# One-hot routing tables in fp16 with the columns innermost, slot lines by rounding, and a new written order, in a fused attention and mixture-of-experts kernel

## The chip, the cores and the metric

The kernel runs on one core of a Trainium2 chip. The metric is the device time of one execution in microseconds (us). TensorE is called PE here, VectorE DVE, ScalarE ACT, GpSimd POOL, and SyncE SP, as in the profile.

## The reference

Eight sequences of 576 tokens go through windowed attention with a linear bias, then through a mixture of eight experts of which each token uses two.

```python
# attention: B, H, S, D = 8, 8, 576, 64, window 128
scores = scale * q @ k.T + slopes * -abs(rel)      # masked outside 0 <= rel < 128
attn = softmax(scores)
x = (attn @ v).reshape(B * S, H * D)               # 4608 x 512
# mixture of experts: E, F = 8, 1024
noisy = x @ w_gate + log1p(exp(x @ w_noise)) * noise
top2 = argpartition(-noisy, 2)[:, :2]
top2_w = softmax of the two
for e in range(E):
    for k in range(2):
        mask = top2[:, k] == e
        h = maximum(x[mask] @ w1[e], 0)
        out[mask] += top2_w[mask, k] * (h @ w2[e])
```

## The kernel before

**Attention and routing.** For each batch of 576 tokens the kernel makes scores of 64-row blocks on PE (line 598), the biased minimum on DVE (line 604), the exponentials on ACT (line 612), transposes on PE (line 619) whose results ACT and DVE copy out (lines 301 and 305, tile pT), and the product with v on PE (line 636). When a batch's attention is done, `route(b)` takes its gate logits, finds the two best experts of each token (lines 850 and 854), ranks the tokens within each expert by a matmul with a triangular matrix (lines 858 and 860), and gives each pair of token and expert a slot number. Slots are kept in lines of 64. To write the token numbers to their slots, `tables` makes two one-hot tables for the 10 pairs (5 token rows times 2 experts) of each partition: one over 80 line numbers (line 893), one over 64 columns (line 897), the second multiplied by the token number (line 901). `list_` adds up ten matmuls of one by the other (line 905), and `scatter` adds the 80x64 result to a list in DRAM. `halves` splits a slot number into line and column by an integer shift and a mask (lines 871 to 875), `next_lines` does the same for the next batch (lines 878 to 881).

**Experts.** Inputs and weights are split into a high and a low fp16 part, and each product is three fp16 matmuls. The first two experts start early: a first wave of blocks (256, 256, 256 and 192 slots of each) is computed as soon as the routing of 2, 4, 6 and 7 batches is complete. The second wave does the rest: the last 256 slots of experts 0 and 1, then experts 2 to 7 in blocks of 512, 512 and up to 192 slots, the 512 ones with seven half-size products in place of eight (lines 1459 and 1496 up, 1659 and 1664 down). Their partial products are copied to tiles named side. Weights of later experts are read, their magnitude is taken (line 1204, ACT), and they are split (lines 301, 303 and 1290) while earlier experts run.

**The order.** No engine chooses its work at run time: each engine's instructions stand in a fixed order. That order is made by a planner inside the kernel (class `Order`) which plays the program through with a cost in us for each piece of work (the first number in `dve(0.98, rank, ...)`) and, of the pieces that are ready on an engine, takes the one with the lowest rank. On PE a piece that keeps the matmul shape of the one before it gets a bonus `STAY`. Work that two engines can do (`either`) goes to the one that is free first, the second at a rank later by an entry of `LATE`. The ranks come from the constants at the top of the file: an attention step of unit t (0 to 159) has rank t plus an entry of `STAGE`, a step of the first wave lies between `FFN0` and `FFN1`, one of the second wave at 1000 and above. A strand that waits for a buffer takes it from a ring, also by rank.

Of the kernel before, what the change touches and what calls it, by code (L numbers as in the profile page):

```python
# [8 lines left out]
F32 = mybir.dt.float32  # L9
# [13 lines left out]
NQ = 5  # L23
# [6 lines left out]
LINE, SPAN = 64, 10  # L30
LINES = 88
# [16 lines left out]
ZERO = 2019.65  # L48
LOAD = 1075.19
VALUES = 1169.98  # L50
GATE = (413.12, 503.1)
GATES = -311.61
ROUTE = -79.16
SCATTER = (-1036.89, -486.7, 213.65)
FFN0, FFN1 = 288.77, 555.18
WEIGHTS = ((918.12, 272.55), (959.66, -236.26))
SEQUENCE = ((0, 0), (0, 1), (1, 0), (1, 1), (0, 2), (1, 2), (0, 3), (1, 3))
TOKENS = -394.6
STAGE = (538.41, 414.48, -338.92, -406.83, 42.73, -373.27, 193.47, -830.41)
MIDDLE = 1630.44  # L60
RESULT = -868.28
WEIGHTS_LATE = 1656.15
SOON = -776.11
LISTED = (36.01, -1817.29)
BIG, PARTS = 1971.78, 542.82
TIGHT = (1, 5, 7)
LATE = (964.06, -1700.75, 837.67, 233.39, 327.65, -1019.18, -417.1, -852.6, 26.68, -922.38, 2132.47, 749.7, 255.16, 538.12)
# [4 lines left out]
REST = -38.3  # L72
PACE = (68.65, -27.38)
HOLD = (-376.19, 197.8)
AHEAD = 1022.78
GATHER_LAG, SCATTER_LAG, LISTED_LAG, TURN_LAG = 4.4, 5.0, 3.0, 4.0
STAY, TURN = -339.23, 0.13
TICK, WARM = 3.413, 1.28
LARGEST = 470.85
# [40 lines left out]
class Order:  # L120
# [141 lines left out]
def attention_moe(ctx: ExitStack, tc: tile.TileContext, qk_, v, vt_, w_gate, w_noise, noise, w12,  # L262
# [83 lines left out]
    steps_ = const.tile([128, E * SPAN], F16, name="steps")  # L346
    numbers = const.tile([128, NQ], F32, name="numbers")
# [8 lines left out]
    lines_ = const.tile([128, 2, E], I32, name="lines")  # L356
# [31 lines left out]
    def set_ups():  # L388
# [9 lines left out]
        def counts_():  # L398
            for t, pattern, first_, step in ((steps_, [[1, E * SPAN]], 0, 0), (numbers, [[64, NQ]], 1, 1),
                                             (spare, [[0, 3], [128, 4]], N, 1), (mine, [[-SPAN, E]], 0, 1)):  # L400
# [325 lines left out]
    def divided(k, low, high, r7):  # L726

        b, y, z = k // NP, k // 2, k % 2
        den = yield (denr, r7)
        if not z:  # L730
            xs_[y] = yield (xr, r7)
            mark(opened[y])
        yield opened[y]
        if not k % NP:
            lts[b] = yield (ltr, r7)
            mark(logged[b])
        yield logged[b]
# [90 lines left out]
    lo_ = ap_.tile([128, NQ, 2], I32, name="lo")  # L828
    si = ap_.tile([128, NQ, 2], I32, name="si")
    hot = [ap_.tile([128, 2 * NQ, c], F16, name=f"hot{c}") for c in (E * SPAN, LINE)]  # L830
# [3 lines left out]
    def route(b):  # L834
# [7 lines left out]
        yield act(0.09, rank, lambda: nc.scalar.activation(u, lg[:, :, 8:16], AF.Abs))  # L842
# [3 lines left out]
        yield act(0.1, rank, lambda: nc.scalar.activation(positive, lg[:, :, 8:16], AF.Relu), False)  # L846
# [18 lines left out]

        def slot_numbers():
            with nc.allow_low_precision(reason="whole numbers below 2^24"):
                V.tensor_reduce(si, oh, axis=AX.X, op=OP.add)

        def halves():  # L870
            V.tensor_scalar(both_i, si, 6, None, op0=OP.arith_shift_right)
            V.tensor_scalar(si, si, LINE - 1, None, op0=OP.bitwise_and)
            V.tensor_copy(d, both_i)
            V.scalar_tensor_tensor(ef, ef, float(SPAN), d, op0=OP.mult, op1=OP.add)
            V.tensor_copy(d, si)

        def next_lines():
            V.tensor_copy(lines_[:, 0], base)
            V.tensor_scalar(lines_[:, 1], lines_[:, 0], 6, None, op0=OP.arith_shift_right)
            V.tensor_copy(line, lines_[:, 1])  # L880
            V.scalar_tensor_tensor(rest_of_line, line, -float(LINE), base, op0=OP.mult, op1=OP.add)
# [7 lines left out]
        def tables(eng, z):  # L889

            if z == 0:
                shape = [128, 2 * NQ, E * SPAN]
                eng.tensor_tensor(hot[0], ef.rearrange("p i k -> p (i k)")[:, :, None].to_broadcast(shape),
                                  steps_[:, None, :].to_broadcast(shape), op=OP.is_equal)
            elif z == 1:
                shape = [128, 2 * NQ, LINE]
                eng.tensor_tensor(hot[1], d.rearrange("p i k -> p (i k)")[:, :, None].to_broadcast(shape),
                                  steps_[:, None, 0:LINE].to_broadcast(shape), op=OP.is_equal)
# [16 lines left out]
        r5, both_i = rk[:, 0:NQ], lo_  # L915
        G = V if b == B - 1 else nc.gpsimd
        rest = [
            (0.09, lambda: V.scalar_tensor_tensor(y_, u, 1.0, y_, op0=OP.subtract, op1=OP.subtract)),
# [9 lines left out]
            (0.39, best), (0.39, where),  # L928
            (0.08, lambda: V.tensor_add(ef, idx[:, :, 0:2], inval)),
            (0.15, lambda: V.tensor_tensor(oh, ef[:, :, :, None].to_broadcast([128, NQ, 2, E]),  # L930
# [20 lines left out]
            (0.5, halves)]  # L951
        onward = [(0.3, next_lines), (0.25, next_places)]
# [26 lines left out]
        yield act(0.1, rank, lambda: nc.scalar.activation(d[:, :, 0], d[:, :, 0], AF.Exp))  # L979
# [11 lines left out]
        yield dve(0.98, rank, lambda: tables(nc.vector, 0))  # L991
        yield dve(0.8, rank, lambda: tables(nc.vector, 1))
        if b == B - 1:
            yield dve(0.8, rank, lambda: tables(nc.vector, 2))
        else:
            yield Op((("POOL", 1.55, rank), ("DVE", 0.8, rank + LATE[10])), lambda g: tables(engine[g], 2), slows=0.4)
        a = yield (tb, rank)
        yield pe(0.4, rank, lambda: list_(a))
        yield dve(0.3, rank, lambda: whole_numbers(a))
# [273 lines left out]
    def difference(o, a, b, op, rank):  # L1273
        return dve(0.08 + o.shape[-1] * 0.00112, rank, lambda: nc.vector.tensor_tensor(o, a, b, op=op))  # L1274
# [70 lines left out]
    def wide_pair(blk, j, xa, xb, tt, end, rank):  # L1345
# [28 lines left out]
        yield dve(1.3, rank, powers)  # L1374
# [19 lines left out]
    def piece(blk, j, q, x, up_, rank, done, lows=None):  # L1394
        c = x.shape[-1]
# [3 lines left out]
        yield dve(0.07 + 0.00115 * c, rank, lambda: nc.vector.scalar_tensor_tensor(lo, x, up_, hi, op0=OP.mult, op1=OP.subtract))  # L1399
# [71 lines left out]
    def ups_of(steps, ranks):  # L1471
        for (blk, f), rank in zip(steps, ranks):
# [10 lines left out]
            us = 3 * (blk.n / 2400 + 0.005)  # L1483
# [192 lines left out]
    def downs_of(steps, ranks):  # L1676
        for (blk, f), rank in zip(steps, ranks):
# [12 lines left out]
            if blk.flip:  # L1690
                for c in range(4):
                    end = yield pe(3 * (blk.n / 2400 + 0.005), rank, lambda: mm2_flipped(blk, f, c, ev[2]), False)
# [374 lines left out]
```

## Time and profile before

| what | value |
|---|---|
| median of 3 runs | 1023.29 us (1021.52 to 1024.88) |
| the profiled execution, its own time | 1020.78 us |
| its span, first to last instruction | 1018.9 us |
| PE busy | 979.8 us (96%), 9734 matmuls |
| DVE busy | 796.2 us (78%), 2733 instructions |
| ACT busy | 564.3 us (55%) |
| POOL busy | 331.0 us (32%) |
| mean granted PE clock | 0.993 |

All durations are of the one profiled execution. Busy time of PE is the union of its matmuls with modelled ends, so a busy PE is not one at its peak; idle PE is certain. "x <- y" in a group of instructions is tile written from tiles read.

### The profile page before, as it was taken

How to read it: one execution, taken by the hardware profiler on the slowest of the kernel's cores; microseconds unless marked ns; L12 is line 12 of the kernel's file. 1: busy time of each engine (PE TensorE's matmuls, PEld its weight loads, DVE VectorE, ACT ScalarE, POOL GpSimd, SP SyncE). 2: the span in 40 equal slices, each digit the busy share in tenths (PEclk: the TensorE clock that was granted, in tenths of full speed). 3: DMA queues.
4: the chain of work that ended last, by engine and by line, in shares of the span. 5: the costliest groups of instructions: out<-in, count | busy, mean ns of one | idle time of the engine just before them, and what ended most of it. 6: DMA issues, size and time to landing. Idle time of an engine off the chain costs nothing.

```text
span 1018.9 us, 25787 instructions
## 1 busy us (share of the span) xinstructions
PE 979.8 (96%) x9734; PEld 701.8 (69%) x9734; DVE 796.2 (78%) x2733; ACT 564.3 (55%) x1367; POOL 331.0 (32%) x442
## 2 busy tenths in 40 slices
PE   7999999999899999979999999999999999999997
PEld 4776777776666689657668666856767686666774
DVE  6989989798997633987799598959978995998240
ACT  6977678485535424664567555634665655544221
POOL 1079432343834224321324142404331232321013
PEclk9999999999999999999999999999999999999999
DMA  8999999794149455895559474949693676638024
GB/s 315 410 312 318 312 336 328 236 295 73 42 93 243 76 81 90 162 218 134 94 109 217 104 130 91 226 74 171 97 236 59 151 147 166 108 65 127 4 40 52
DMA packets 175534, 166.59 MB, mean 164 GB/s; under 512 B 128928, under 2 KB 139248, under 8 KB 175408
## 3 DMA queue, kind: packets, MB, share of 16 engines
q1 hardware_dynamic: 157888, 125.59, 45.9%
q0 software_dynamic: 17520, 39.34, 21.8%
q8 instruction: 77, 1.26, 0.5%
q14 instruction: 49, 0.40, 0.1%
HBM read 95.11 MB, written 40.91 MB: 133 GB/s over the span
## 4 chain that ended last, share of the span: by engine, by line
PE 79%; DVE 13%; POOL 2%; DMA 2%; issue 2%; ACT 1%; SPq 0%; POOLq 0%; DVEq 0%; ACTq 0%
PE bank L1659 31%; PE bank L1496 18%; PE bank L1459 12%; PE bank L636 5%; PE bank L1664 4%; PE bank L598 3%; PE bank L619 3%; DVE bhl L1611 1%; DVE p L604 1%; DMA qk<-in_qk_dram 1%; DVE side L1599 1%; DVE held L1290 1%; POOL held L1287 1%; DVE x L748 1%; DVE pT L305 1%
## 5 line engine op out<-in xcount | busy, mean ns | idle before, releaser
L1659 PE MATMUL bank<-held,bhh 128*128 128x512 f16 x734 | 218.4, 379 | 2.6 <-ACT bhh L1618 2.6
L1496 PE MATMUL bank<-bx,held 128*128 128x256 f16 x1824 | 210.5, 273 | 6.8 <-ACT side L301 6.3
L1796 POOL DMA_INDIRECT out_dram<-yo,ix x58 | 96.0, 1655 | 338.0 <-ACT yo L301 281.6
L1496 PEld LDWEIGHTS <-held 128*128 128x128 f16 x1824 | 178.7, 98 | 33.2 <-issue 8.2
L1659 PE MATMUL bank<-held,bhl 128*128 128x512 f16 x367 | 139.1, 379 | 1.5 <-DVE bhl L1611 1.5
L1659 PEld LDWEIGHTS <-bhh 128*128 128x128 f16 x784 | 75.8, 98 | 88.9 <-ACT bhh L1618 4.1
L1459 PE MATMUL bank<-ax,held 128*128 128x256 f16 (+6 forms) x1380 | 133.9, 252 | 2.0 <-DVE ahl L1650 1.5
L1459 PEld LDWEIGHTS <-held 128*128 128x128 f16 x1380 | 115.8, 98 | 17.7 <-issue 3.8
L612 ACT ACTIVATE p<-p,nm 128x192 f32<-128x192 f32 (+2 forms) x288 | 103.7, 427 | 22.4 <-DVE nm L604 21.6
L301 ACT ACTIVATE xt<-xg,fit 128x512 f16<-128x512 f32 (+5 forms) x93 | 62.6, 677 | 60.3 <-DVE fit L1366 27.2
L1618 ACT ACTIVATE bhh<-side 128x512 f16<-128x512 f32 x69 | 42.4, 627 | 94.8 <-DVE side L1599 93.2
L604 DVE CUSTOM_DVE_ANT_0 p<-bank,bias 128x192 f32<-128x192 f32 (+2 forms) x288 | 81.8, 327 | 5.5 <-PE bank L598 4.8
L301 ACT ACTIVATE held<-held,wsc 128x512 f16<-128x512 f32 x93 | 63.3, 713 | 28.9 <-DVE held L1274 14.3
L636 PE MATMUL bank<-vraw,pT 64*64 64x81 f32 (+1 forms) x2048 | 76.7, 240 | 1.6 <-DVE pT L305 0.6
L636 PEld LDWEIGHTS bank<-vraw,pT 64*64 64x64 f32 (+1 forms) x2048 | 68.5, 137 | 10.2 <-issue 2.0
L1338 POOL DMA_INDIRECT xg<-xs_dram,ix x48 | 51.8, 1080 | 70.6 <-DVE xt L1399 36.8
L619 PE MATMUL bank<-ident,p 128*128 128x128 f32 x416 | 68.1, 286 | 6.3 <-ACT pT L301 2.8
L1659 PEld LDWEIGHTS <-bhl 128*128 128x128 f16 x392 | 38.3, 98 | 48.9 <-DVE bhl L1611 2.9
L598 PE MATMUL bank<-qk 64*64 64x192 f32 (+2 forms) x1152 | 65.7, 326 | 6.5 <-DMA qk<-in_qk_dram 5.1
L1290 DVE SCALAR_TENSOR_TENSOR held<-held,wsc,held 128x512 f16<-128x512 f32 x96 | 70.9, 767 | 0.0
L1204 ACT ACTIVATE junk<-held 128x512 bf16<-128x512 f32 x104 | 65.1, 626 | 6.2 <-DMA held<-in_w_dram 4.3
L619 PEld LDWEIGHTS bank<-ident,p 128*128 128x128 f32 x416 | 45.7, 142 | 32.3 <-ACT pT L301 7.6
(284 smaller groups left out, 1793.1 us busy)
## 6 DMA issues: line engine op xcount, KB each, us to landing
held<-in_w_dram SPq DMA_DIRECT2D x61, 512.0 KB
qk<-in_qk_dram SPq DMA_DIRECT2D x31, 576.0 KB
vraw<-in_v_dram SPq DMA_DIRECT2D x16, 810.0 KB
out_dram<-xg SPq DMA_DIRECT2D x10, 1024.0 KB
vt<-in_vt_dram SPq DMA_DIRECT2D x16, 576.0 KB
xs_dram<-x SPq DMA_DIRECT2D x16, 320.0 KB
xs_dram<-x SPq DMA_DIRECT2D x16, 256.0 KB
bx<-xt SPq DMA_TRANSPOSE x96
```

Source lines behind the costliest of these rows:

```text
L301: nc.scalar.activation(o, i, AF.Copy, **kw)
L598: nc.tensor.matmul(s[j % 2][half:half + 64, o:o + c], qk[rows, j * 64:j * 64 + 64], qk[rows, k1 - c:k1], start=True, stop=True)
L604: nc.vector.tensor_tensor_reduce(out=p[:, place(j):place(j) + c], in0=s[z][:, o:o + c], in1=bias4[:, g, z, 192 - c:192], scale=-0.125, sca ...
L612: nc.scalar.activation(pv, pv, AF.Exp, bias=nm[:, z:z + 1], scale=-1.0)
L619: nc.tensor.transpose(t[:, z * 128:z * 128 + 128], p[:, a * 128:a * 128 + 128], ident)
L636: nc.tensor.matmul(o[z * 64:z * 64 + 64, c:c + VC], pt[rows, slot, from_:from_ + 64], t[rows, block, hh], start=(o is first_, z) not in be ...
L1204: nc.scalar.activation(junk, raws_flat(t, z), AF.Abs, accum_out=wam[:, e % 2, z, f:f + 1])
L1290: nc.vector.scalar_tensor_tensor(lo, t, sc, hi, op0=OP.mult, op1=OP.subtract)
L1459: nc.tensor.matmul(t[:, 0:blk.n], wp[:, c], blk.x[:, x + c, 0:blk.n], start=c == 0 and z == 0, stop=c == 3 and z == 2)
L1496: nc.tensor.matmul(t[:, a % 2 * HALF:a % 2 * HALF + HALF], wp, blk.x[:, x], start=first_, stop=False, skip_group_check=True)
L1659: nc.tensor.matmul(blk.y[j][0:r], h[:, cs], wp, start=f == 0 and m == 0, stop=f == 7 and m == 2)
L1796: ins = nc.gpsimd.indirect_dma_start(out=out, out_offset=bass.IndirectOffsetOnAxis(ap=blk.ix[0:r, j:j + 1], axis=0), in_=t[0:r, 0:DM], in_ ...
```

## The change

**Tables.** `row` and `col`, the line and column number of each pair, are now fp16, and so are the counting table `steps_` and the token numbers; the counting table is held expanded over the ten pairs (800 elements where it was 80). The pair index becomes the innermost axis of the tables, `[128, c, 10]` where it was `[128, 10, c]`, so that both inputs of the compare are contiguous on it, and the ten matmuls of `list_` read their operands with a step of ten elements. **Slot lines.** The line of a slot is found by adding and subtracting 1.5 x 2^23 in fp32, with no integers: four instructions per batch where there were five, and three where there were four for the next batch. **Order.** Nearly all rank constants change, and the planner's costs of many pieces (the factor 1.03 on late DVE work goes, too).

```diff
+WHOLE = 1.5 * 2.0 ** 23
-FFN0, FFN1 = 288.77, 555.18
+FFN0, FFN1 = 985.65, 988.51
-STAGE = (538.41, 414.48, -338.92, -406.83, 42.73, -373.27, 193.47, -830.41)
+STAGE = (762.91, 398.43, -692.29, -873.25, -99.37, -122.48, 294.62, -1402.25)
-STAY, TURN = -339.23, 0.13
+STAY, TURN = -180.73, 0.13
...
-        elif e == "DVE" and self.now > FFN1:
-            us *= 1.03
...
-    steps_ = const.tile([128, E * SPAN], F16, name="steps")
-    numbers = const.tile([128, NQ], F32, name="numbers")
+    steps_ = ap_.tile([128, E * SPAN, 2 * NQ], F16, name="steps")
+    numbers = const.tile([128, NQ, 2], F16, name="numbers")
...
+    row, col = (ap_.tile([128, 2 * NQ], F16, name=name) for name in ("row", "col"))
+    hot = [ap_.tile([128, c, 2 * NQ], F16, name=f"hot{c}") for c in (E * SPAN, LINE)]
...
+        def whole_lines(o, i):
+            V.tensor_scalar(o, i, 1.0 / LINE, 0.5 / LINE - 0.5, op0=OP.mult, op1=OP.add)
+            V.tensor_scalar(o, o, WHOLE, WHOLE, op0=OP.add, op1=OP.subtract)
...
         def halves():
-            V.tensor_scalar(both_i, si, 6, None, op0=OP.arith_shift_right)
-            V.tensor_scalar(si, si, LINE - 1, None, op0=OP.bitwise_and)
-            V.tensor_copy(d, both_i)
-            V.scalar_tensor_tensor(ef, ef, float(SPAN), d, op0=OP.mult, op1=OP.add)
-            V.tensor_copy(d, si)
+            row_, col_ = (x.rearrange("p (i k) -> p i k", k=2) for x in (row, col))
+            whole_lines(ln, si)
+            V.scalar_tensor_tensor(row_, ef, float(SPAN), ln, op0=OP.mult, op1=OP.add)
+            V.scalar_tensor_tensor(col_, ln, -float(LINE), si, op0=OP.mult, op1=OP.add)
...
         def next_lines():
-            V.tensor_copy(lines_[:, 0], base)
-            V.tensor_scalar(lines_[:, 1], lines_[:, 0], 6, None, op0=OP.arith_shift_right)
-            V.tensor_copy(line, lines_[:, 1])
+            whole_lines(line, base)
...
+            if z < 2:
+                shape = list(hot[z].shape)
+                eng.tensor_tensor(hot[z], (row, col)[z][:, None, :].to_broadcast(shape), steps_[:, 0:shape[1]], op=OP.is_equal)
             else:
-                h = hot[1].rearrange("p (i k) c -> p i (k c)", k=2)
-                eng.tensor_tensor(h, h, numbers[:, :, None].to_broadcast([128, NQ, 2 * LINE]), op=OP.mult)
+                eng.tensor_tensor(hot[1], hot[1], numbers.rearrange("p i k -> p (i k)")[:, None, :].to_broadcast([128, LINE, 2 * NQ]),
+                                  op=OP.mult)
...
-                nc.tensor.matmul(a[0:E * SPAN, 0:LINE], hot[0][:, z], hot[1][:, z], start=z == 0, stop=z == 2 * NQ - 1)
+                nc.tensor.matmul(a[0:E * SPAN, 0:LINE], hot[0][:, :, z], hot[1][:, :, z], start=z == 0, stop=z == 2 * NQ - 1)
...
-        yield dve(0.98, rank, lambda: tables(nc.vector, 0))
-        yield dve(0.8, rank, lambda: tables(nc.vector, 1))
+        yield dve(0.55, rank, lambda: tables(nc.vector, 0))
+        yield dve(0.45, rank, lambda: tables(nc.vector, 1))
```

## Rows read from the trace of the kernel before

**Rows 1.** Windows by stage; columns: stretch, its length, busy time (instructions) by engine, clock, DMA.
```profile
0.00:10.00 10.00, 4.94 (x62) 3.14 (x62) 6.06 (x35) 7.22 (x19) 3.26 (x23) 1.00 0.70 216
10.00:20.00 10.00, 7.95 (x84) 5.26 (x78) 7.26 (x46) 6.14 (x17) 0.14 (x1) 0.83 1.02 360
20.00:300.00 280.00, 267.73 (x4187) 197.91 (x4186) 249.65 (x1283) 190.41 (x548) 128.56 (x199) 0.99 0.81 259
300.00:440.00 140.00, 140.00 (x1143) 105.20 (x1142) 89.80 (x278) 63.44 (x154) 43.33 (x49) 1.00 0.63 130
440.00:460.00 20.00, 13.86 (x100) 10.18 (x99) 17.97 (x52) 14.03 (x34) 5.47 (x5) 0.91 0.97 218
460.00:1006.00 546.00, 539.99 (x4125) 375.00 (x4124) 425.08 (x1043) 281.87 (x593) 145.64 (x160) 1.00 0.62 119
1006.00:1019.00 13.00, 5.32 (x50) 5.07 (x47) 0.37 (x2) 1.22 (x3) 4.60 (x6) 0.87 0.64 85
```

**Rows 2.** Windows, the ten of 20 to 300 us with most idle PE, one and their sum.
```profile
260.00:270.00 10.00, 8.54 (x108) 6.19 (x106) 9.67 (x39) 6.28 (x15) 9.52 (x10) 1.00 0.27 61
...
sum 100.00, PE 89.33 PEld 65.08 DVE 94.67 ACT 70.38 POOL 58.85; mean PE 8.93 PEld 6.51 DVE 9.47 ACT 7.04 POOL 5.89
```

**Rows 3.** Waits of PE from 20 to 300 us: us in total, times, longest.
```profile
PE bank L619 <- ACT pT L301: 2.8, 6, 0.8
PE bank L619 <- DVE pT L305: 2.4, 4, 1.1
```

**Rows 4.** Timeline at 444 to 453 us: start, us, engine, line, operation.
```profile
444.62 0.62 ACT L1204 ACTIVATE junk<-held 128x512 bf16<-128x512 f32 x1
...
445.79 1.47 PE L1496 MATMUL bank<-bx,spare 128*128 128x256 f16 x12
...
450.06 0.63 ACT L1204 ACTIVATE junk<-held 128x512 bf16<-128x512 f32 x1
...
452.12 1.06 ACT L301 ACTIVATE side<-bank 128x512 f32<-128x512 f32 x2
...
452.75 2.71 PE L1496 MATMUL bank<-bx,held 128*128 128x256 f16 x12 [5.48 <-ACT side L301]
```

**Rows 5.** The tile hot: duration in ns, least, median, most.
```profile
L893 DVE TENSOR_TENSOR hot<-ef,steps x8: 975/982/1919, 76.7 to 299.8; 128x800 f16<-128x800 f32 x8
L897 DVE TENSOR_TENSOR hot<-d,steps x8: 761/816/973, 78.9 to 301.5; 128x640 f16<-128x640 f32 x8
L901 POOL TENSOR_TENSOR hot<-hot,numbers x6: 1254/1256/1256, 81.3 to 247.3; 128x640 f16<-128x640 f16 x6
L901 DVE TENSOR_TENSOR hot<-hot,numbers x2: 818/818/818, 283.3 to 302.9; 128x640 f16<-128x640 f16 x2
```

**Rows 6.** DVE groups by line and shape, 0 to 330 us: busy us, mean ns.
```profile
L871 DVE TENSOR_SCALAR lo<-si 128x10 int32<-128x10 int32 x8 | 2.6, 327 | 0.2
...
L875 DVE CAST d<-si 128x10 f32<-128x10 int32 x8 | 2.0, 252 | 0.3
...
L872 DVE TENSOR_SCALAR si<-si 128x10 int32<-128x10 int32 x8 | 1.8, 230 | 0.3
...
L873 DVE CAST d<-lo 128x10 f32<-128x10 int32 x8 | 1.7, 207 | 0.0
...
L874 DVE SCALAR_TENSOR_TENSOR ef<-ef,d 128x10 f32<-128x10 f32 x8 | 1.4, 171 | 0.3
```

**Rows 7.** Timeline of PE at 85 us, the ten products of one list.
```profile
85.27 0.54 PE L905 MATMUL bank<-hot,hot 128*80 128x64 f16 x10
```

**Rows 8.** Timeline of POOL at the start.
```profile
2.68 0.21 POOL L401 IOTA steps<- 128x80 f16 x1
```

**Rows 9.** Windows at the hand-over and at two later changes of expert.
```profile
450.00:460.00 10.00, 7.25 (x53) 5.85 (x53) 8.11 (x24) 5.60 (x13) 2.24 (x2) 0.83 0.95 203
550.00:560.00 10.00, 8.22 (x67) 6.21 (x64) 9.49 (x29) 8.54 (x23) 4.04 (x3) 1.00 1.17 227
...
930.00:940.00 10.00, 8.42 (x41) 3.54 (x39) 9.06 (x23) 3.61 (x7) 0.00 (x0) 1.00 0.41 79
```

More of the change, by code (lines that the diff above doesn't have):

```diff
@@ L71 @@
 DMA_LAG = 4.0
[L72 to L75, printed above, removed]
+REST = -113.98
+PACE = (44.6, -12.0)
+HOLD = (24.18, 221.19)
+AHEAD = 776.98
 GATHER_LAG, SCATTER_LAG, LISTED_LAG, TURN_LAG = 4.4, 5.0, 3.0, 4.0
-STAY, TURN = -339.23, 0.13
+STAY, TURN = -180.73, 0.13
 TICK, WARM = 3.413, 1.28
-LARGEST = 470.85
+LARGEST = 2707.67
 WIDES, SIDE = 4, 4
@@ L398, in counts_ @@
         def counts_():
-            for t, pattern, first_, step in ((steps_, [[1, E * SPAN]], 0, 0), (numbers, [[64, NQ]], 1, 1),
+            for t, pattern, first_, step in ((steps_, [[1, E * SPAN], [0, 2 * NQ]], 0, 0), (numbers, [[64, NQ], [0, 2]], 1, 1),
                                              (spare, [[0, 3], [128, 4]], N, 1), (mine, [[-SPAN, E]], 0, 1)):
@@ L841, in route @@
         positive = oh2.rearrange("p i k e -> p (i k e)")[:, 0:NQ * E].rearrange("p (i e) -> p i e", e=E)
-        yield act(0.09, rank, lambda: nc.scalar.activation(u, lg[:, :, 8:16], AF.Abs))
+        yield act(0.18, rank, lambda: nc.scalar.activation(u, lg[:, :, 8:16], AF.Abs))
         yield act(0.13, rank, lambda: nc.scalar.activation(y_, u, AF.Exp, scale=-1.0))
@@ L845, in route @@
         yield act(0.13, rank, lambda: nc.scalar.activation(l, u, AF.Ln), False)
-        yield act(0.1, rank, lambda: nc.scalar.activation(positive, lg[:, :, 8:16], AF.Relu), False)
+        yield act(0.18, rank, lambda: nc.scalar.activation(positive, lg[:, :, 8:16], AF.Relu), False)
         def best():
@@ L927, in route @@
         choose = [
-            (0.39, best), (0.39, where),
-            (0.08, lambda: V.tensor_add(ef, idx[:, :, 0:2], inval)),
-            (0.15, lambda: V.tensor_tensor(oh, ef[:, :, :, None].to_broadcast([128, NQ, 2, E]),
+            (0.39, best), (0.62, where),
+            (0.13, lambda: V.tensor_add(ef, idx[:, :, 0:2], inval)),
+            (0.25, lambda: V.tensor_tensor(oh, ef[:, :, :, None].to_broadcast([128, NQ, 2, E]),
                                            iota8[:, None, None, :].to_broadcast([128, NQ, 2, E]), op=OP.is_equal)),
@@ L950, in route @@
             (0.2, slot_numbers),
-            (0.5, halves)]
-        onward = [(0.3, next_lines), (0.25, next_places)]
+            (0.75, halves)]
+        onward = [(0.5, next_lines), (0.5, next_places)]
         def chain(steps, wait):
@@ L978, in route @@
         end = yield pe(0.2, rank, ranks, False)
-        yield act(0.1, rank, lambda: nc.scalar.activation(d[:, :, 0], d[:, :, 0], AF.Exp))
+        yield act(0.2, rank, lambda: nc.scalar.activation(d[:, :, 0], d[:, :, 0], AF.Exp))
         yield end
@@ L990, in route @@
         spawn(gates_out(b, rank))
-        yield dve(0.98, rank, lambda: tables(nc.vector, 0))
-        yield dve(0.8, rank, lambda: tables(nc.vector, 1))
+        yield dve(0.55, rank, lambda: tables(nc.vector, 0))
+        yield dve(0.45, rank, lambda: tables(nc.vector, 1))
         if b == B - 1:
-            yield dve(0.8, rank, lambda: tables(nc.vector, 2))
+            yield dve(0.45, rank, lambda: tables(nc.vector, 2))
         else:
-            yield Op((("POOL", 1.55, rank), ("DVE", 0.8, rank + LATE[10])), lambda g: tables(engine[g], 2), slows=0.4)
+            yield Op((("POOL", 1.55, rank), ("DVE", 0.45, rank + LATE[10])), lambda g: tables(engine[g], 2), slows=0.4)
         a = yield (tb, rank)
         yield pe(0.4, rank, lambda: list_(a))
-        yield dve(0.3, rank, lambda: whole_numbers(a))
+        yield dve(0.35, rank, lambda: whole_numbers(a))
         put(tb, a)
@@ L1273, in difference @@
     def difference(o, a, b, op, rank):
-        return dve(0.08 + o.shape[-1] * 0.00112, rank, lambda: nc.vector.tensor_tensor(o, a, b, op=op))
+        return dve(0.34, rank, lambda: nc.vector.tensor_tensor(o, a, b, op=op))
     def turn_over(both, t):
@@ L1373, in wide_pair @@
         yield either(1.25, 1.3, rank, LATE[13], largest)
-        yield dve(1.3, rank, powers)
+        yield dve(1.15, rank, powers)
         mark(blk.weighed)
@@ L1394, in piece @@
     def piece(blk, j, q, x, up_, rank, done, lows=None):
-        c = x.shape[-1]
+        c = HALF if lows is None and q == 3 else DM
         xt = yield (xtr, rank)
@@ L1691, in downs_of @@
                 for c in range(4):
-                    end = yield pe(3 * (blk.n / 2400 + 0.005), rank, lambda: mm2_flipped(blk, f, c, ev[2]), False)
+                    end = yield pe(3 * (blk.n / 2400 + 0.0035), rank, lambda: mm2_flipped(blk, f, c, ev[2]), False)
                     if f == 7:
```

63 lines of the change are left out of this document (26 added, 37 removed).

## The prediction

> **What bounds the kernel now.** I read three views in this order. First the windows by stage [rows 1]: TensorE (PE) is busy in 979.8 of 1018.9 us, so 39 us of the span are idle PE. They lie unevenly. The first 20 us lose 7.1 us and the last 13 us lose 7.7 us; 20 to 300 us, where attention, routing and the first expert blocks run mixed, lose 12.3; 300 to 440 loses none; 440 to 460 loses 6.1 at a mean granted clock of 0.91; 460 to 1006 loses 6.0. A kernel that is PE-bound in this way gains only where PE idles, so the change can't be worth what it saves on another engine, only what of it ends a PE wait.
>
> Second, the ten windows of 10 us in the mixed stage where PE idles most [rows 2]. They hold 10.7 of that stage's 12.3 us of idle PE, and in them VectorE (DVE) is busy 94.67 of 100 us. In the other 180 us of the stage it is busy 154.98 (249.65 less 94.67), 86%. PE idles where DVE is fullest. The waits agree: in that stage PE waits longest for the copies that ACT and DVE make of its transposes, 2.8 and 2.4 us [rows 3]. DVE is the limit of those places, and the tables of the change are DVE work in exactly that stage.
>
> Third, the hand-over at 440 to 460 [rows 4]. PE stops 5.48 us until ACT has copied two products into "side". ACT did that copy at 452.12; from 444.62 on it ran six magnitude passes (line 1204) over weights of a later expert, the last begun at 450.06. The products were ready soon after 447.26, when the last matmuls that PE had begun ended (445.79 + 1.47). So here the written order on ACT is wrong for the times that came about; DVE, too, is full, 17.97 of the 20 us [rows 1].
>
> **The change part by part.** *Tables.* Per batch DVE makes a row table of 800 elements in 982 ns and a column table of 640 in 816 ns (medians, [rows 5]); that is (982-816)/160 = 1.04 ns an element and 150 ns fixed. The change gives all operands fp16 and keeps the last axis contiguous in both inputs. Two prices bound it. The nearest row is the multiply on DVE, fp16 into fp16 with an fp32 factor: 818 ns for 640 elements [rows 5], no faster than the fp32 compare; by it the tables save nothing. At half the time per element they cost 150 + 416 = 0.57 and 150 + 333 = 0.48 us, a saving of 0.41 + 0.34 = 0.75 us a batch, 6.0 over eight, and 0.7 more for the two multiplies that DVE makes. The diff's planner charges 0.55 and 0.45, close to the second, and the row has one fp32 operand where the change has none; I take the half, and keep zero for the range. The Trainium skill, "VectorE: DVE Perf Modes", section "The perf-mode tier table", says that tensor_tensor runs at twice its fp32 rate when every operand is 16-bit; no run here shows it yet, the mixed row neither for nor against, and by it the saving would be the 6.7 us.
>
> *Slot lines.* Five small DVE instructions of 327, 230, 207, 171 and 252 ns a batch (1.19 us, [rows 6]) become four: two tensor_scalar at no more than the 327 ns of the row and two like the 171 ns, at most 1.00. That saves 0.19 or more, 1.5 us over eight batches. The lines for the next batch go from four instructions to three; one less at the 171 ns of line 874 is 1.2 us over seven. Together 2.7 us.
>
> So DVE is freed of 9.4 us between 76.7 and 304 us (2.7 if the fp16 form is no faster). What that gives the end: at most 9.4, if each lies under an idle PE; nothing if each lies under first-wave matmuls that PE has queued. The eight batches spread over the stage and the idle PE is in ten windows that make up 100 of 280 us, but it is there that DVE is the limit. I take half: -4.7 us.
>
> *PE.* The ten products of a list take 0.54 us per batch [rows 7]; their operands are now read with a step of 20 bytes. At no cost 0, at twice the time 4.3 us over eight batches; nothing in the trace has such a step. I take 0, since only 80 of 9734 matmuls are concerned, and keep the 4.3.
>
> *GpSimd.* Its multiply (1256 ns, six batches, [rows 5]) has the same 640 elements: 0. The counting table at the start grows from 80 to 800 elements: 213 ns [rows 8], so at most ten times that, 1.9 us more, once; it lies under POOL's own idle (busy 3.26 of the first 10 us, [rows 1]), so 0, and 1.9 if what POOL does after it were waited for.
>
> *The order.* Every rank and most planner costs change, so every engine's queue is interleaved anew, the DMA issues of SP and POOL too. The ranks say one thing plainly: scores had rank 538 to 698 and first-wave expert steps 289 to 555, so expert steps went first; now scores have 763 to 922 and the steps 986 to 989, so attention goes first and the steps fill gaps, with the bonus for staying in one matmul shape cut from 339 to 181. Attention's softmax thus asks for DVE earlier, and the first wave is left as a reserve for PE. It can gain what idles for order alone: 6.1 us of idle at the hand-over and 1.7 of half clock (0.83 over the 10 us from 450, [rows 9]), 7.8 together. The planner's times now come from the trace, which is what the misplaced ACT copy lacked; but DVE is full there too, so I take half, -3.9. Of the 6.0 us in 460 to 1006 and of the start (DMA) and tail (last products and scatters) I take nothing.
>
> Sum: -4.7 - 3.9 = -8.6 us. The profiled execution took 1020.78 us (span 1018.9 and 1.9 around it), so 1012.2; the median of the runs, 1023.3, is 2.5 above it, so **1015 us** after.
>
> **The rivals.** *The order gets most of it* (17%). If DVE relief and order empty the ten windows (-10.7) and the hand-over (-7.8): 1005 us; with the small waits after it too (-6.0), 999. For it: PE's own work would allow it. Against: planned order never met the trace so well before; 6 us of waits survive even in the regular second stage.
>
> *PE pays for the step* (7%). The strided operands double the list's products, and they stand in PE's queue in the mixed stage: +4.3 on the forecast, 1019 us. For it: nothing in rows, the 0.54 us stands for contiguous operands. The Trainium skill, "SBUF — State Buffer", section "Door 1: The DMA port swizzle", says that an engine reads at full rate only while it stays inside a 16-byte line; with steps of 20 bytes every element would leave its line. No run here shows it for PE.
>
> *No difference* (16%): the freed DVE time lies under queued expert matmuls and the hand-over stays: 1020 to 1026 us. For it: in 300 to 440 PE is full whatever DVE does.
>
> *Slower* (22%): the hand-over's wait comes back at the changes of expert. Each later change (near 555 and 935, [rows 9]) now loses 1.6 to 1.8 us, with DVE over 9 of 10 us busy around it: one weight split or one copy placed too late makes a wait as at 452, 5.5 us plus 1.7 of clock, 7.2. From the tables' -4.7 alone, with the old hand-over kept, one more such wait gives 1026, two give 1033. It decides from the first: one is slower by 0.3%. For it: every queue is new, and the second stage, now almost free of waits, has the more to lose.
>
> **How the numbers follow.** About 0.3%, 3 us, is what a measurement of this kernel tells from no change (its runs span 3.4 us). Forecast 38% (1009 to 1020), most of the order's chance 17%, strided PE 7%, no difference 16%, slower 22%. Faster: 38 + 17 + 7 = 62%, same 16%, slower 22%. The range goes from 1003, just under the case that empties windows and hand-over, to 1028, past one extra wait; two waits and the 999 are the 2 in 10 left out.
>
> **What would show it.** Right: the row and column tables near 0.57 and 0.48 us; DVE some 7 to 9 us less in total; idle PE in 20 to 300 us down from 12.3 to about 8; at the hand-over a wait for "side" under 3 us. Wrong: tables still at 0.98 and 0.82; the list's ten products at 1 us; or PE full as before at the old places but with new waits of 5 us in 460 to 1006 and a clock of 0.83 behind them. Then the order, not the tables, set the time.

## The result and the profile after

The changed kernel takes 1013.95 us (median of 4 runs, 1011.98 to 1015.32); the kernel before took 1022.62 beside it. The ratio on record is 0.9889, 95% interval 0.9854 to 0.9923; it is not the ratio of the two medians, which is 0.9915. On another chip it was 0.9912 (0.9897 to 0.9927). The profiled execution took 1015.32 us, the longest of the four; its span is 1013.5, 5.4 us under that of before. A second profile of the same kernel, on the other chip (after_again), has a span of 1008.2 us: a single profile is good to a few us only.

Windows of the changed kernel by stage, columns as in [rows 1]:

```profile
0.00:10.00 10.00, 5.07 (x62) 3.13 (x62) 8.00 (x37) 7.18 (x19) 5.84 (x23) 1.00 0.70 219
10.00:20.00 10.00, 7.85 (x84) 5.35 (x78) 7.06 (x44) 6.63 (x19) 0.13 (x1) 0.83 1.02 347
20.00:300.00 280.00, 268.45 (x4165) 202.79 (x4164) 234.95 (x1230) 188.14 (x535) 122.38 (x193) 0.99 0.79 255
300.00:440.00 140.00, 139.39 (x1127) 104.20 (x1125) 89.39 (x314) 62.31 (x160) 46.12 (x51) 1.00 0.63 133
440.00:460.00 20.00, 17.14 (x127) 12.04 (x125) 19.72 (x49) 13.39 (x31) 7.43 (x4) 1.00 0.87 190
460.00:1006.00 546.00, 544.93 (x4183) 381.47 (x4181) 430.14 (x1059) 283.00 (x589) 146.09 (x164) 1.00 0.62 122
1006.00:1014.00 8.00, 0.00 (x0) 0.00 (x0) 0.00 (x0) 0.40 (x1) 1.54 (x2) 0.66 0.32 48
```

PE is busy for 982.8 us where it was 979.8, so idle PE fell from 39.1 to 30.7 us, and 3 us of that went into more busy PE. The stages say where PE idles less. The hand-over (440 to 460) idles 2.9 us, not 6.1, at full clock where it was 0.91. The second stage (460 to 1006) idles 1.1 us, not 6.0. The mixed stage, where the tables are, idles 11.6 us where it was 12.3, though DVE is busy 14.7 us less in it. So the idle time that went lies in the two stages in which no table is made. after_again agrees: 2.7 us in 440 to 460 at full clock, and 1.0 from 460 to 1000. In the second stage of before, two of PE's waits (us in total, times, longest) are gone in the changed kernel:

```profile
PE bank L1659 <- ACT bhh L1618: 2.6, 3, 1.5
PE bank L1659 <- DVE bhl L1611: 1.5, 3, 1.0
```

The tile hot of the changed kernel, durations in ns (least, median, most), answers to [rows 5]:

```profile
L899 PEld LDWEIGHTS <-hot x80: 216/234/248, 83.9 to 317.3; 128*80 128x80 f16 x80
L899 PE MATMUL bank<-hot,hot x80: 286/320/324, 84.0 to 317.4; 128*80 128x64 f16 x80
L892 DVE TENSOR_TENSOR hot<-row,steps x8: 511/565/569, 76.6 to 313.2; 128x800 f16<-128x800 f16 x8
L892 DVE TENSOR_TENSOR hot<-col,steps x8: 477/484/1045, 77.4 to 314.4; 128x640 f16<-128x640 f16 x8
L894 POOL TENSOR_TENSOR hot<-hot,numbers x6: 1315/1321/1327, 78.9 to 242.9; 128x640 f16<-128x640 f16 x6
L894 DVE TENSOR_TENSOR hot<-hot,numbers x2: 485/490/495, 291.6 to 315.1; 128x640 f16<-128x640 f16 x2
```

The compares take 565 and 484 ns, where they took 982 and 816, and the multiply on DVE 490 where it took 818. But the matmuls that read these tables are slower: a weight load of 234 ns and a product of 320. Ten products of one list, on the timeline of PE, were 0.54 us in [rows 7] and are now:

```profile
84.04 1.55 PE L899 MATMUL bank<-hot,hot 128*80 128x64 f16 x10
```

That is 1.01 us more of PE in each of eight batches, 8.1 us. The busy time of these matmuls alone (PE, PEld), before and after, says the same:

```profile
0.00:330.00 330.00, 4.36 (x80) 4.12 (x80) 0.99 0.81 255
...
0.00:330.00 330.00, 12.41 (x80) 11.99 (x80) 0.99 0.79 247
```

So PE's other matmuls together take 970.4 us (982.8 less 12.4), where they took 975.4 (979.8 less 4.4). The span's 5.4 us are thus 8.4 of idle PE and 5.0 of matmul time gained, and 8.0 lost to the ten products. At most 1.7 of the 5.0 is the clock at the hand-over (0.83 over 10 us, [rows 9]); where the new order saves the rest was not tried.

The counting table of 800 elements costs more at the start than ten times the 0.21 us of [rows 8], and an instruction of DVE that runs beside it, 0.23 us in the kernel before, takes 2.19:

```profile
2.69 2.69 POOL L399 IOTA steps<- 128x800 f16 x1
...
3.33 2.19 DVE L383 TENSOR_SCALAR before<-spare 128x128 bf16<-128x128 f32 x1
```

PE does not wait for it: it is busy 5.07 us of the first 10, 4.94 before. The slot lines, DVE groups by line (busy us, mean ns; [rows 6]):

```profile
L876 DVE SCALAR_TENSOR_TENSOR col<-ln,si 128x10 f16<-128x10 f32 x8 | 2.3, 285 | 0.0
...
L867 DVE TENSOR_SCALAR ln<-ln 128x10 f32<-128x10 f32 x8 | 1.8, 223 | 0.3
...
L875 DVE SCALAR_TENSOR_TENSOR row<-ef,ln 128x10 f16<-128x10 f32 x8 | 1.4, 171 | 0.3
...
L866 DVE TENSOR_SCALAR ln<-si 128x10 f32<-128x10 f32 x8 | 1.3, 158 | 0.1
```

Four instructions of 285 + 223 + 171 + 158 = 837 ns stand where five took 1187. At the hand-over the timeline (start, us, engine, line) has the copy to side in nearly its right place; [rows 4] had 5.48 us here:

```profile
452.24 1.47 PE L1490 MATMUL bank<-bx,spare 128*128 128x256 f16 x12
...
452.83 0.63 ACT L1198 ACTIVATE junk<-held 128x512 bf16<-128x512 f32 x1
...
453.46 1.06 ACT L300 ACTIVATE side<-bank 128x512 f32<-128x512 f32 x2
...
454.08 1.47 PE L1490 MATMUL bank<-bx,held 128*128 128x256 f16 x12 [0.37 <-ACT side L300]
```

PE's last products before it were issued at 452.24, the copy starts at 453.46, and PE waits 0.37 us.

### The profile page after: what moved, and what is told of

Read it like the earlier page. It is cut to its first block, busy times and chain, and to the rows that moved or that the text cites. A ratio compares the mean times of both kernels' runs of the same rounds, so it can differ in the third digit from the quotient of the medians.

```text
span 1013.5 us, 25811 instructions
## 1 busy us (share of the span) xinstructions
PE 982.8 (97%) x9734; PEld 709.0 (70%) x9734; DVE 789.3 (78%) x2727; ACT 561.1 (55%) x1350; POOL 329.5 (33%) x438
## 4 chain that ended last, share of the span: by engine, by line
PE 82%; DVE 9%; POOL 3%; issue 2%; DMA 2%; ACT 1%; another core or an unknown queue 0%; SPq 0%; POOLq 0%; ACTq 0%; DVEq 0%
PE bank L1653 29%; PE bank L1490 19%; PE bank L1453 11%; PE bank L634 6%; PE bank L596 5%; PE bank L1658 4%; PE bank L617 4%; POOL held L1281 1%; DVE held L1284 1%; DMA qk<-in_qk_dram 1%; PE bank L899 1%; PE bank L523 1%; DVE xt L1393 1%; DVE held L1268 1%; POOL held L1282 1%
## 5 line engine op out<-in xcount | busy, mean ns | idle before, releaser
L1790 POOL DMA_INDIRECT out_dram<-yo,ix x58 | 98.1, 1691 | 312.5 <-ACT yo L300 299.6
L300 ACT ACTIVATE xt<-xg,fit 128x512 f16<-128x512 f32 (+4 forms) x98 | 65.5, 677 | 58.5 <-DVE fit L1360 27.2
L300 ACT ACTIVATE held<-held,wsc 128x512 f16<-128x512 f32 x89 | 60.9, 715 | 49.5 <-DVE held L1268 26.8
L634 PEld LDWEIGHTS bank<-vraw,pT 64*64 64x64 f32 (+1 forms) x2048 | 67.4, 135 | 12.3 <-issue 4.8
L1612 ACT ACTIVATE ahh<-bank 128x256 f16<-128x256 f32 (+1 forms) x63 | 23.3, 370 | 83.4 <-PE bank L1653 41.0
```

Of the source, the lines that this page charges most:

```text
L300: nc.scalar.activation(o, i, AF.Copy, **kw)
L634: nc.tensor.matmul(o[z * 64:z * 64 + 64, c:c + VC], pt[rows, slot, from_:from_ + 64], t[rows, block, hh], start=(o is first_, z) not in be ...
L1612: nc.scalar.activation(o, i, AF.Relu)
L1790: ins = nc.gpsimd.indirect_dma_start(out=out, out_offset=bass.IndirectOffsetOnAxis(ap=blk.ix[0:r, j:j + 1], axis=0), in_=t[0:r, 0:DM], in_ ...
```

## The experiments

In each kernel below the instructions of every engine were held in the order of the kernel that it is derived from, except where the order is what is tried; only the table and slot-line instructions differ. Four kernels ran on each chip with the kernel before beside them, so ratios to it are compared, not times. 0.1% is 1.02 us. The ratios are those on record; they differ from the ratios of the medians by up to 0.13%, so a difference of that size between two kernels says nothing.

| kernel | order | tables | slot lines | median us | ratio to before (95%) |
|---|---|---|---|---|---|
| changed | new | fp16, columns innermost | new | 1013.95, 1011.01 | 0.9889 (0.9854 to 0.9923), 0.9912 (0.9897 to 0.9927) |
| e1_tables | old | fp16, columns innermost | new | 1024.60 | 1.0039 (1.0017 to 1.0060) |
| e5_tables_pairs | old | fp16, contiguous pairs | new | 1017.29 | 0.9971 (0.9957 to 0.9984) |
| e2_order | new | old | old | 1013.15 | 0.9934 (0.9916 to 0.9953) |
| e11_lines | new | old | new | 1006.59 | 0.9871 (0.9850 to 0.9892) |
| e4_dtype | new | fp16, old layout | new | 1007.21 | 0.9882 (0.9860 to 0.9904) |
| e3_pairs | new | fp16, contiguous pairs | new | 1005.61 | 0.9853 (0.9831 to 0.9875) |
| e8_stationary | new | rows strided | new | 1012.72 | 0.9938 (0.9914 to 0.9961) |
| e9_moving | new | columns strided | new | 1011.03 | 0.9905 (0.9887 to 0.9923) |
| e10_thrice | new | as e3, products made thrice | new | 1011.78 | 0.9908 (0.9888 to 0.9928) |
| e6_costs | new costs, old ranks | as e3 | new | 1047.50 | 1.0274 (1.0240 to 1.0307) |
| e7_ranks | old costs, new ranks | as e3 | new | 1013.46 | 0.9943 (0.9922 to 0.9965) |

**The two halves of the change, each alone.** e1_tables is the kernel before with all lines of the diff that concern tables and slot lines, and with the old constants and costs:

```diff
-    hot = [ap_.tile([128, 2 * NQ, c], F16, name=f"hot{c}") for c in (E * SPAN, LINE)]
+    hot = [ap_.tile([128, c, 2 * NQ], F16, name=f"hot{c}") for c in (E * SPAN, LINE)]
...
         yield dve(0.98, rank, lambda: tables(nc.vector, 0))
```

> The new tables and slot lines in the order of the kernel before: every engine's instructions stand as before, only the tables, the slot lines and the ten products of a list differ. Theory A (the prediction: DVE relief of some 9 us, half of it reaches the end): about -4.7 us against the kernel before, 1018. Theory B (PE pays: the ten products take 1.55 us in the changed kernel, 0.54 before, so about 1 us more in each of eight batches, and this eats the DVE relief): between -2 and +4 us, and idle PE from 20 to 300 us smaller while busy PE grows by 8 us.

Theory A fell. The tables and slot lines alone make the kernel slower, by 0.39%. DVE has its relief (790.0 us busy, 796.2 before), and PE idles less where the tables are made (9.4 us in 20 to 300, 12.3 before), but PE is busy 8.4 us more (988.2 us). The ten products cost what they cost in the changed kernel, on PE's timeline:

```profile
83.54 1.55 PE L901 MATMUL bank<-hot,hot 128*80 128x64 f16 x10
```

At the hand-over this kernel, with the old order, still waits (us in total, times, longest) as the kernel before did:

```profile
PE bank L1492 <- ACT side L302: 5.5, 1, 5.5
```

e2_order is the changed kernel with the old table and slot-line code, in the changed kernel's order:

```diff
-            whole_lines(ln, si)
+            V.tensor_scalar(both_i, si, 6, None, op0=OP.arith_shift_right)
...
-                eng.tensor_tensor(hot[z], (row, col)[z][:, None, :].to_broadcast(shape), steps_[:, 0:shape[1]], op=OP.is_equal)
+                eng.tensor_tensor(hot[0], ef.rearrange("p i k -> p (i k)")[:, :, None].to_broadcast(shape),
+                                  steps_[:, None, :].to_broadcast(shape), op=OP.is_equal)
```

> The old tables and slot lines in the order of the changed kernel. Theory A: the order alone is worth about -3.9 us against the kernel before, 1019, mostly at the hand-over. Theory B: the order is worth the whole gain or more, -9 to -14 us (1009 to 1014), since here the ten products cost 0.54 us again, and DVE has the old 9 us more.

The order alone gives -0.66%, some 6.7 us: more than theory A's 3.9, less than theory B's 9 to 14. Part of what it lost is at the hand-over: PE idles 4.1 us in 440 to 460 there, at a clock of 0.91. The timeline shows why:

```profile
439.70 0.60 PE L1657 MATMUL bank<-held,ahh 128*128 128x512 f16 x2
...
445.24 0.72 ACT L299 ACTIVATE xt<-xg,fit 128x512 f16<-128x512 f32 x1 [3.92 <-DMA bx<-xt]
445.86 0.36 ACT L1616 ACTIVATE ahh<-bank 128x256 f16<-128x256 f32 x1
...
446.28 0.61 PE L1657 MATMUL bank<-held,ahh 128*128 128x512 f16 x2 [2.85 <-ACT ahh L1616]
```

PE's wait of 2.85 us ends with ACT's relu of a block (line 1616), and that relu stood in ACT's queue behind a conversion into xt that waited 3.92 us for the DMA transpose that was still reading that buffer. It is the fault of [rows 4] in another place: an instruction that waits holds up one that PE needs. The second stage, in contrast, has its gain: PE idles 0.95 us from 460 to 1000, as in the changed kernel, 6.0 in the kernel before.

**Is it the step of the operands?** e3_pairs keeps the changed kernel's order and writes each line and column number twice, so that the compare's innermost axis is a pair of contiguous fp16 in both inputs and the tables are contiguous along the columns, as before:

```diff
-    row, col = (ap_.tile([128, 2 * NQ], F16, name=name) for name in ("row", "col"))
-    hot = [ap_.tile([128, c, 2 * NQ], F16, name=f"hot{c}") for c in (E * SPAN, LINE)]
+    row, col = (ap_.tile([128, 2 * NQ, 2], F16, name=name) for name in ("row", "col"))
+    hot = [ap_.tile([128, 2 * NQ, c], F16, name=f"hot{c}") for c in (E * SPAN, LINE)]
...
+                c = hot[z].shape[2] // 2
+                shape = [128, 2 * NQ, c, 2]
+                eng.tensor_tensor(hot[z].rearrange("p z (c t) -> p z c t", t=2), (row, col)[z][:, :, None, :].to_broadcast(shape),
+                                  steps_[:, 0:2 * c].rearrange("p (c t) -> p c t", t=2)[:, None].to_broadcast(shape), op=OP.is_equal)
...
-                nc.tensor.matmul(a[0:E * SPAN, 0:LINE], hot[0][:, :, z], hot[1][:, :, z], start=z == 0, stop=z == 2 * NQ - 1)
+                nc.tensor.matmul(a[0:E * SPAN, 0:LINE], hot[0][:, z], hot[1][:, z], start=z == 0, stop=z == 2 * NQ - 1)
```

> The changed kernel in its own order, with the tables stored with the columns contiguous again, and each line and column number written twice, so that the compare's innermost axis is a contiguous pair of fp16 in both inputs. If the step of the operands is what makes the ten products slow, they fall from 1.55 to about 0.54 us and PE's busy time by 8 us; the compares stay at 0.57 and 0.49 us if a contiguous pair is enough for the double rate. Theory B: 4 to 8 us faster than the changed kernel (1006 to 1010). Theory A (DVE is the limit where PE idles, PE has room): within 2 us of the changed kernel.

The tile hot of e3_pairs:

```profile
L901 PEld LDWEIGHTS <-hot x80: 117/123/190, 84.2 to 308.4; 128*80 128x80 f16 x80
L901 PE MATMUL bank<-hot,hot x80: 192/203/261, 84.4 to 308.5; 128*80 128x64 f16 x80
L893 DVE TENSOR_TENSOR hot<-row,steps x8: 514/565/567, 76.9 to 305.2; 128x800 f16<-128x800 f16 x8
L893 DVE TENSOR_TENSOR hot<-col,steps x8: 474/484/1042, 77.8 to 306.4; 128x640 f16<-128x640 f16 x8
L897 POOL TENSOR_TENSOR hot<-hot,numbers x6: 1253/1255/1257, 79.2 to 238.8; 128x640 f16<-128x640 f16 x6
L897 DVE TENSOR_TENSOR hot<-hot,numbers x2: 484/488/492, 284.4 to 307.1; 128x640 f16<-128x640 f16 x2
```

Load and product are back at 123 and 203 ns, and the compares keep their 565 and 484: a pair of contiguous elements is enough for that rate. It has the lowest ratio of all kernels here, 0.9853, though not clear of e4_dtype and e11_lines below; after_again, the changed kernel on the chip of the second four, had 0.9912. Against it that is 0.6%, 6 us, with intervals that don't meet (with that of the first result, 0.9854 to 0.9923, it does). Theory B held.

> The changed kernel, unaltered, beside the three others of this chip. Theory B (the ten products cost PE 8 us): near 0.989 of the kernel before, about 4 us or more above the version with contiguous tables in the same order (0.985 on the chip of the last runs). Theory A: no difference from that version beyond its interval.

e5_tables_pairs does the same in the order of the kernel before:

> The order of the kernel before, with the fp16 tables, but stored contiguously (each number written twice): the tables' DVE relief without the price on PE. Theory A (half of the DVE relief reaches the end): 4 to 5 us faster than the kernel before. Theory B (PE pays the 8 us in the kernel with the new tables in the old order, which was 4 us slower than before): 8 us less than that, again 4 us faster than before. Theory C (the relief lies under queued matmuls): within 2 us of before.

Beside e1_tables only the layout differs, and with it the counting table at the start, of 80 elements again; PE is busy 4.40 and 4.73 us in the first 10 us of the two, so no cost of that table shows at PE. The ten products are at

```profile
82.84 0.54 PE L903 MATMUL bank<-hot,hot 128*80 128x64 f16 x10
```

The ratio falls from 1.0039 to 0.9971: the step cost 0.68%, 6.9 us at the end, for its 8.1 us of PE. Without it the tables and slot lines are worth 0.29% in the old order, 3.0 us (1.6 to 4.4 by the interval), below theory A's 4 to 5.

**Which operand.** e8_stationary strides only the row table (PE's weights), e9_moving only the column table (what streams); the other stays contiguous.

```diff
-    hot = [ap_.tile([128, 2 * NQ, c], F16, name=f"hot{c}") for c in (E * SPAN, LINE)]
+    hot = [ap_.tile([128, c, 2 * NQ] if z == 0 else [128, 2 * NQ, c], F16, name=f"hot{c}") for z, c in enumerate((E * SPAN, LINE))]
...
-                nc.tensor.matmul(a[0:E * SPAN, 0:LINE], hot[0][:, z], hot[1][:, z], start=z == 0, stop=z == 2 * NQ - 1)
+                nc.tensor.matmul(a[0:E * SPAN, 0:LINE], hot[0][:, :, z], hot[1][:, z], start=z == 0, stop=z == 2 * NQ - 1)
```

> Order of the changed kernel, contiguous fp16 tables, but the row table (the weights of the ten products) with its columns innermost, read by PE with a step of 20 bytes; the column table stays contiguous. If the weights alone make the products slow: their load takes 235 ns again, ten products about 1.5 us, and the end comes 5 us later than with both contiguous. If each operand carries its own part: load 235 and product 203 ns, ten in between.

> The other half: the column table (the operand that streams) with a step of 20 bytes, the row table contiguous. If the streamed operand makes the products slow: 320 ns each and about 1.5 us for ten, load at 123 ns. If only the weights matter: products at 203 ns, ten in 0.54 us, and the end as with both contiguous.

The tile hot of e8_stationary:

```profile
L906 PEld LDWEIGHTS <-hot x80: 213/234/238, 85.8 to 313.9; 128*80 128x80 f16 x80
L906 PE MATMUL bank<-hot,hot x80: 193/304/308, 85.9 to 314.0; 128*80 128x64 f16 x80
```

One list of it on PE's timeline:

```profile
85.94 1.48 PE L906 MATMUL bank<-hot,hot 128*80 128x64 f16 x10
```

The tile hot of e9_moving, where the load stays near 123 ns:

```profile
L906 PEld LDWEIGHTS <-hot x80: 117/136/136, 83.6 to 312.9; 128*80 128x80 f16 x80
L906 PE MATMUL bank<-hot,hot x80: 275/296/298, 83.7 to 313.0; 128*80 128x64 f16 x80
```

And one list of it:

```profile
83.74 1.32 PE L906 MATMUL bank<-hot,hot 128*80 128x64 f16 x10
```

Either operand alone makes ten products take 1.3 to 1.5 us, both together 1.55. The costs don't add: 0.94 and 0.78 us alone, 1.01 together. That fits a load and a product that run side by side, the slower one setting the pace, but no run shows this directly. Neither "the weights alone" nor "each carries a part" was right. At the end the two stand 0.85% (e8_stationary) and 0.52% (e9_moving) above e3_pairs. That e8_stationary is above even the changed kernel, with both operands strided (0.9938 and 0.9912), is not clear of noise: their intervals overlap.

**Is it PE time as such?** e10_thrice makes the ten contiguous products of e3_pairs three times over, the last ten giving the result:

```diff
-            for z in range(2 * NQ):
+            for z in 3 * list(range(2 * NQ)):
```

> Order of the changed kernel, both tables contiguous, and the ten products of each list made three times over (the last ten give the result): 1.1 us more of PE per batch, without any step. Theory B (PE time in these places goes one to one to the end, whatever makes it): 6 to 8 us slower than with ten products, near 0.992 of before, like the changed kernel itself. If PE has room there: within 2 us of 0.985.

The thirty take:

```profile
84.06 1.30 PE L901 MATMUL bank<-hot,hot 128*80 128x64 f16 x30
```

That is 0.76 us more per batch, 6.1 over eight (expected were 1.1 each: ten more products behind the first add only 0.38). The end moves from 0.9853 to 0.9908, 0.55% or 5.6 us. Three comparisons thus give 0.7 to 0.9 us at the end per us of PE time put into these places: 6.0 of 8.1 (after_again against e3_pairs), 6.9 of 8.1 (e1_tables against e5_tables_pairs) and 5.6 of 6.1 here, where no step is involved. By the intervals each end is uncertain by some 3 us. Theory B held within that.

**Is it DVE time?** e4_dtype gives all operands fp16, but broadcasts the number over the innermost axis; e11_lines takes the old fp32 tables and only the new slot lines. Both are in the changed kernel's order, with contiguous tables.

```diff
-                eng.tensor_tensor(hot[z].rearrange("p z (c t) -> p z c t", t=2), (row, col)[z][:, :, None, :].to_broadcast(shape),
+                eng.tensor_tensor(hot[z], (row, col)[z][:, :, 0:1].to_broadcast(shape),
```

> The changed kernel in its own order, all operands fp16, tables in the old layout, the number broadcast over the innermost axis. If the type alone gives DVE its double rate, the compares take 0.57 and 0.49 us, and the kernel equals the one with pairs; if the contiguous innermost axis is needed, they take 0.98 and 0.82, and the kernel lies between that with the old tables and that with pairs.

> Order of the changed kernel, old fp32 tables, but the slot lines by rounding: between the kernel with old tables and old slot lines (0.993, with a wait of 2.9 us of PE for ACT at the hand-over) and the one with fp16 tables at the same cost (0.988, without it). If the saved DVE instructions are what counts: 0.988. If that wait comes and goes with any shift of the times before it: 0.988 or 0.993, to be seen by whether PE waits at 440 to 450 us.

The compares of e4_dtype, from its tile hot:

```profile
L892 DVE TENSOR_TENSOR hot<-row,steps x8: 930/981/985, 75.2 to 304.5; 128x800 f16<-128x800 f16 x8
L892 DVE TENSOR_TENSOR hot<-col,steps x8: 815/819/1643, 76.4 to 306.2; 128x640 f16<-128x640 f16 x8
```

So the type alone gives nothing; at full price on DVE (792.4 us busy, 785.5 in e3_pairs) the kernel is at 0.9882, and e11_lines at 0.9871. By the ratios the 6.9 us of DVE that the pairs save bring 0.18 to 0.29%, 2 to 3 us; the medians of e4_dtype and e3_pairs, which ran on one chip, are 1.6 us apart, and the intervals overlap. That the relief is worth anything in the new order is therefore not shown. e11_lines and e2_order differ only in the slot lines, 2 us of DVE's busy time (792.2 and 794.1), and yet by 0.63%, 6.4 us. The hand-over makes part of it: in e11_lines ACT's conversion into xt finds its buffer free, and the relu behind it isn't held up (timeline, ACT):

```profile
435.90 0.71 ACT L300 ACTIVATE xt<-xg,fit 128x512 f16<-128x512 f32 x1
438.15 0.38 ACT L1615 ACTIVATE ahh<-bank 128x256 f16<-128x256 f32 x1 [1.54 <-PE bank L1456]
```

The hand-over of e11_lines begins before 440 us, so the stretch that holds both is 430 to 460 (first e2_order, then e11_lines):

```profile
430.00:460.00 30.00, 25.88 (x181) 18.05 (x180) 26.48 (x66) 18.92 (x45) 9.16 (x9) 0.94 1.16 189
...
430.00:460.00 30.00, 27.11 (x205) 19.79 (x204) 29.57 (x75) 21.80 (x50) 8.41 (x5) 1.00 0.94 195
```

PE idles 2.9 us there, not 4.1, at full clock, not 0.94: 1.2 us of idle and about 1.8 of clock, 3.0 of the 6.4 us. In these two profiles another part lies in the first 20 us, before any slot line is computed: PE is busy 12.4 us of them at a clock of 0.91 in e2_order, 14.8 at 1.00 in e11_lines. There the changed kernel differs from itself nearly as much: 12.9 us at 0.91 in its first profile, 14.3 at 1.00 in after_again. What the slot lines are worth in the new order thus stays open. What made the transpose of e2_order late, 130 us after the last slot line, was not tried.

**Costs or ranks?** Both kernels have the tables of e3_pairs. e6_costs has the planner's new costs with the old constants, e7_ranks the new constants with the old costs:

```diff
-STAGE = (762.91, 398.43, -692.29, -873.25, -99.37, -122.48, 294.62, -1402.25)
+STAGE = (538.41, 414.48, -338.92, -406.83, 42.73, -373.27, 193.47, -830.41)
```

> Contiguous fp16 tables, the planner's new costs, the old ranks. If the costs read from the trace make the better order (the prediction's reason: times that fit the chip put no copy in a wrong place), this is close to the version with new costs and new ranks, about 0.985 of before, and the 5.5 us wait for side at the hand-over is gone. If the ranks make it, this is near 0.995 and the wait is still there.

> Contiguous fp16 tables, the planner's old costs, the new ranks. If the costs make the order better: 0.995 of before or worse, with a wait of several us at some change of expert. If the ranks make it: about 0.985.

e6_costs fits neither case of its expectation. Old ranks with the new costs give the slowest kernel, 1.0274. Two of its windows (columns as in [rows 1]) show PE idle, at a mean granted clock of 0.50 and 0.83:

```profile
220.00:240.00 20.00, 12.29 (x123) 8.64 (x122) 12.24 (x74) 9.77 (x27) 6.99 (x12) 0.50 0.74 202
...
460.00:480.00 20.00, 13.46 (x85) 9.04 (x83) 17.62 (x47) 11.07 (x26) 5.56 (x5) 0.83 1.10 235
```

The first is attention without first-wave work behind it: not one matmul of the first wave (lines 1455 and 1655) stands in it, 68 do in 180 to 200, and PE's longest waits are 3.3 and 2.4 us, both for DVE. The second is a hand-over with the wait for side again, 4.9 us. New ranks with the old costs (e7_ranks) give 0.9943, near the case "the costs make the order better", and 0.9% above new ranks with new costs (0.9853). But with the same tables both old give 0.9971 (e5_tables_pairs): new costs alone make it 3% slower, new ranks alone do not make it faster clear of noise, both together make it 1.2% faster. So neither part makes the order good; the ranks are good together with the costs that came with them. How either was found is not on record.

## Why the prediction was right, and where it was not

It gave 1015 us and faster; 1014 and faster came out. But its two terms were both off, and the errors cancelled: the tables and slot lines, forecast at -4.7 us, cost 4.0 in the old order (1.0039), and the order, forecast at -3.9, gave some 13 (1.0039 to 0.9912). That the sum came out right is luck. One of its own signs of being wrong came true, too: "the list's ten products at 1 us". They took 1.55.

- *What bounds the kernel.* PE, as said, and in a direction that I priced too low: PE time added in the mixed stage costs the end 0.7 to 0.9 us per us. But that the kernel gains only where PE idles is not so: 5.0 us came from less matmul time in the new order, at most 1.7 of it the clock. And freeing DVE ended less of the idle PE in 20 to 300 us than forecast, from 12.3 to about 8: it is 11.6 in the changed kernel (10.0 in after_again), and with the old order 9.4 (e1_tables) and 9.8 (e5_tables_pairs), where 3.1 us of new idle stand in 300 to 440.
- *The compares* were priced right: 0.57 and 0.48 us forecast, 565 and 484 ns measured. The Trainium skill, "VectorE: DVE Perf Modes", section "Mode 2×_1P", asks for 16-bit operands with a step of one. The trace agrees: with a step of zero on one input, in e4_dtype, they take 981 and 819. *Slot lines:* 0.19 us a batch or more was forecast, 0.35 measured. In total 9.4 us of DVE were forecast; busy DVE fell by 6.9 us in the changed kernel and by 11.2 in e5_tables_pairs (785.0 us).
- *"I take half: -4.7."* Too much. In the old order with contiguous tables it was -3.0 us (1.6 to 4.4); in the new order 2 to 3 by the ratios for the tables alone, not clear of noise.
- *"I take 0" for the step on PE* is the step of the argument that failed. It was +8.1 us of PE, nearly twice the bound that I kept, and 6 to 7 us at the end. The rival to which I gave 7% was the mechanism; I bounded it by doubling since no row had such a step, and argued that 80 matmuls are few. The Trainium skill, "SBUF — State Buffer", section "Door 1: The DMA port swizzle", says that each access that crosses to a new 16-byte line pays a penalty. The trace agrees with its direction: 123 ns of load and 203 of product became 234 and 320. It gives no amount for PE.
- *GpSimd.* The counting table was to take at most 1.9 us more; it took 2.5 more (2.69 and 0.21), and DVE's instruction beside it 2.0 more. At the end it cost nothing that the first 10 us show, as forecast.
- *The order, -3.9.* Mis-sized by three: with equal tables it is worth 1.0039 to 0.9912 (strided) or 0.9971 to 0.9853 (contiguous), 12 to 13 us. With the old tables and slot lines it was 6.7 (e2_order), with a wait at the hand-over. The hand-over gave 3.3 us of idle and 1.7 of clock, more than the half that I took, and 460 to 1006, for which I took nothing, gave 4.9; the matmuls other than the ten products take 5.0 us less (at most 1.7 of it the clock), a term that the sum does not have.
- *Its reason*, that planner times from the trace place the copies better, is not shown: the new costs with the old ranks made the kernel 2.7% slower than before.
- *The slower rival* (a wait at a change of expert) did not come in the changed kernel. Waits of that kind came at the hand-over of e2_order (2.85 us) and e6_costs (4.9). That they come because the order met other durations than those it was made for is argued, not shown.

## What to carry to other kernels

An operand layout is shared by its writer and its readers: before the axis that is contiguous is changed to speed the engine that writes, count every read of the engine that bounds the kernel. Both could have it here: writing each number twice kept DVE's faster compare and PE's contiguous read, and gave the lowest ratio. An order written out in advance was good here only together with the costs that it came with: judge it with them, and look, in each change of stage, for an instruction that waits in front of one that the bounding engine needs.

## What the runs showed of the hardware

- PE reading 64 or 80 fp16 columns with a step of 20 bytes: ten load and product pairs take 1.55 us in place of 0.54; with only the weights strided 1.48, with only the streamed operand 1.32.
- DVE's fp16 compare of 800 elements takes 565 ns when the innermost axis is contiguous in both inputs, even if it is only two elements long, and 981 when one input is broadcast along it.
- GpSimd's multiply of 640 fp16 took 1321 ns with the token numbers along the innermost axis of ten, and 1255 with pairs.
- While GpSimd wrote a counting table of 128x800 fp16 (2.69 us), a DVE instruction on 128x128 elements took 2.19 us, 0.23 in the kernel before.
